# A retention and MLP kernel on one core: the Q tile holds both batches of a stream, and the weight slabs start from other loads

## The chip, the core and the metric

The kernel runs on one core of one Trainium2 chip. Its engines are TensorE (PE, matrix products; PEld is its weight load), VectorE (DVE), ScalarE (ACT), GpSimd (POOL) and SyncE (SP, which here only issues transfers). Data moves between DRAM and the on-chip memories through DMA queues that 16 DMA engines serve. The metric is the device time of one execution in microseconds (us), taken as the median of several runs.

## The reference

The inputs q, k and v have the shape 8 batches x 8 heads x 576 tokens x 64, in fp32. The second half is an MLP over all 4608 tokens.

```python
scores = 1/sqrt(64) * np.matmul(q, k.transpose(0, 1, 3, 2))
gamma = 1.0 - 2.0 ** (-5.0 - np.arange(H))
rel = pos[:, None] - pos[None, :]
Dmat = np.where(rel >= 0, gamma[:, None, None] ** rel[None, :, :], 0.0)
ret = (scores * Dmat) @ v
x = ret.transpose(0, 2, 1, 3).reshape(B * S, H * D)       # 4608 x 512
h = x @ w_in                                              # 512 x 2048
g = h * np.cos(h)
out = g @ w_out                                           # 2048 x 512, fp32
```

The decay matrix factors: gamma^(i-j) = gamma^i x gamma^-j. So the kernel scales row i of Q by gamma^i/8 (the table WQ) and row j of V by gamma^-j (the table WV), and only the causal mask is left for the scores.

## The kernel before

**Tiling.** A sequence of 576 tokens is cut into 9 chunks of 64. The 8 batches are split into two streams, x and y (numbers 0 and 1), and each stream goes through two generations: a unit (stream, k) with k from 0 to 17 is one chunk of the two batches that the stream has in that generation. Between chunks a state of keys times values is carried on in PSUM, so a chunk needs only its own keys and the state. Two units of a stream fill a part of one MLP tile; there are 9 MLP tiles (j from 0 to 8) of 512 tokens each.

**Loads of a pair of chunks.** `kv_tile` (L474 on) loads 128 tokens (two chunks) of K for each of two batches into `stgk` (L493, 256 KB each), and V into `stgv`. Each row is one token, and each piece of a row is one head's 64 fp32 numbers, 256 bytes. K is cast to bf16 into `natk` (L471) and V times WV goes to `natv` (L506), on ACT and DVE for the first tiles (`fast`) and on POOL for the others. K is then turned, with TensorE against the identity IDN (`tpe` L568, `tph` L586 for the last chunk of a sequence) or with a transposing DMA (`txb`, in generation 1).

**Q tiles.** `q_tile` (L528 on, load L543, multiply L550) has one tile per batch. In mode "n" the tile holds 128 tokens of one batch, one token in each of the 128 partitions, 256 KB in pieces of 256 bytes. In mode "p" it holds 256 tokens of one batch, two neighbouring tokens in each partition, 512 KB in pieces of 512 bytes. Chunk 8 is a mode "n" tile of 64 tokens. The product with WQ goes to `qnat`, its transpose to `qt`. In generation 0, chunks 0 to 3 are mode "n" and chunks 4 to 7 mode "p"; in generation 1 chunks 0 to 7 are mode "p". The pool of `stgq` has two slots.

**Sessions.** `session` (L608 on) takes the units that are due. On TensorE it issues scores (L627), new states (L636), the part of the output from the state (L645) and the part from the chunk itself (L654). DVE multiplies the scores by the mask (`pt`, L716), ACT copies outputs to `xt`, the MLP's input (L470).

**MLP.** `mlp1` issues x times w_in in groups of four matmuls (L756), then the sine (L764, ACT) and the product (L767, DVE). The second product is `plain2` (L793) for tile 0; for the others it is `wino2` (L879), a Strassen-Winograd form with fewer matmuls, whose operands DVE adds up (L840) from weights summed beforehand (`wsums`).

**Weights.** `load_w` (L736, L740) issues four slabs of w_in (512 KB each, 4 of the 16 column blocks of the MLP) and four of w_out on POOL's queue. The order of the w_in slabs is 0, 2, 1, 3. All eight wait for a gate: the landing of the second K load of stream y's first tile. The loads of chunks 2 and 3 (`GATE`) wait in turn: those of stream x for w_out slab 1, those of stream y for w_out slab 3.

**Order of the work.** `Graph` is a list scheduler: it takes the tasks with their priorities, planned durations, planned DMA times and buffer pools, and writes out one fixed stream of instructions per engine. It also models the fetching of TensorE's code: each block of 256 instructions becomes available FETCH (5500 ns) after it is asked for. Into gaps that the plan sees on TensorE before the first MLP matmul, `warm` (L412) puts dummy matmuls. On the chip the streams run in order, joined by semaphores.

Of the kernel before, what the change touches and what calls it, by code (L numbers as in the profile page):

```python
# [6 lines left out]
ALU = mybir.AluOpType  # L7
AF = mybir.ActivationFunctionType
F32 = mybir.dt.float32
# [120 lines left out]
class Graph:  # L130


    BACKLOG, FETCH, MARGIN = 2500, 5500, 60

    def __init__(self, pools):
        self.tasks, self.wr, self.rd = [], {}, {}
# [61 lines left out]
    def run(self, dma_rate):  # L198
# [65 lines left out]
        while n < len(self.tasks):  # L264
# [21 lines left out]
            if t.ni:  # L286
                while (len(got) + 0.74) * 256 <= count + t.ni:
                    at = s + t.dur * max(0, (len(got) + 0.74) * 256 - count) / t.ni
                    got.append(max([at] + [x - self.FETCH + 1500 for x in got[-1:]]) + self.FETCH)
                count += t.ni  # L290
            if t.port:
                port_free[e] = s + t.dur
# [30 lines left out]
class Kernel:  # L323
# [13 lines left out]
        [((), ((0, 4),)), (((0, 4),), ((0, 5), (1, 4))), (((0, 5), (1, 4)), ((0, 6), (1, 5))),  # L337
         (((0, 6), (1, 5)), ((0, 7), (1, 6)))])
    PLAIN = (0,)
    NOXBAR = set(range(7))  # L340
    PERIOD, T0, T1 = 28800, 18000, 32000

    def __init__(self, nc, es, q, k, v, w_in, w_out, out):
        self.nc = nc
        self.P = Prog(nc, es)
        self.src = [q.tensor, k.tensor, v.tensor]
        self.w_in, self.w_out, self.out = w_in.tensor, w_out.tensor, out.tensor
        sb = nc.alloc_sbuf_tensor
# [5 lines left out]
        self.WQ = sb("wq", [128, 56], F32)  # L354
# [4 lines left out]
        self.IQ = sb("iq", [128, 56], F32)  # L359
        self.IV = sb("iv", [128, 48], F32)  # L360
        self.LV = sb("lv", [128, 48], F32)
        self.LQ = sb("lq", [128, 56], F32)
# [55 lines left out]
    def constants(self):  # L418
# [5 lines left out]
        P.add("pool", lambda e: e.iota(ap(self.IV, 48, 0, 128, 40, [1, 8]), [[0, 8]], base=448,  # L424
                                       channel_multiplier=1, allow_small_or_imprecise_dtypes=True), w=[("iv", 1)])
        for m, r0 in self.WQS:
            o, nx = self.wq(m, r0), 2 if m == "p" else 1
            P.add("pool", lambda e, o=o, nx=nx, r0=r0: e.iota(
                ap(self.IQ, 56, 0, 128, o, [1, 8 * nx]), [[1, nx], [0, 8]], base=CH * r0, channel_multiplier=nx,
                allow_small_or_imprecise_dtypes=True), w=[("iq", o)])  # L430
        P.add("pool", lambda e: e.affine_select(self.IDN.ap(), self.ONE.ap(), pattern=[[1, 128]],
                                                compare_op=ALU.is_equal, fill=0.0, base=0,
                                                channel_multiplier=-1), r=["one"], w=["idn"])
        for h in range(H):
            P.add("dve", lambda e, h=h: e.memset(ap(self.LQ, 56, 0, 128, h, [8, 7]), lng[h]), w=[("lq", h)])
        for h in range(H):
            P.add("dve", lambda e, h=h: e.memset(ap(self.LV, 48, 0, 128, h, [8, 6]), -lng[h]), w=[("lv", h)])
        P.add("dve", lambda e: e.memset(self.CLN.ap(), math.log(1.0 / 8.0)), w=["cln"])
        P.add("dve", lambda e: e.memset(self.CPI.ap(), math.pi / 2), w=["cpi"])
        P.add("dve", lambda e: e.tensor_tensor(self.LQ.ap(), self.IQ.ap(), self.LQ.ap(), ALU.mult),  # L440
              r=[("iq", self.wq(*k)) for k in self.WQS] + [("lq", h) for h in range(H)], w=["lqx"])
# [77 lines left out]
        load("stgk", 1)  # L519
        return load, casts  # L520

    QT = {0: [("n", 0, 2), ("n", 2, 2), ("p", 4, 4), ("n", 8, 1)], 1: [("p", 0, 4), ("p", 4, 4), ("n", 8, 1)]}
    WQS = [("n", 0), ("n", 2), ("p", 4), ("n", 8), ("p", 0)]

    def wq(self, mode, r0):
        o = 0
        for m, r in self.WQS:
            if (m, r) == (mode, r0):  # L528
                return o
            o += 16 if m == "p" else 8  # L530

    def q_tile(self, x, gen, i, xbar, fast, gate=()):

        mode, r0, nr = self.QT[gen][i]
        wide = mode == "p"
        n, m = (64 if nr == 1 else 128), (2 if wide else 1) * D
        for b2 in range(2):
            t = {k: Buf(k) for k in ("stgq", "qnat")}
            t["qt"] = Buf("qt" if nr > 1 else "q8")
            for r in range(r0, r0 + nr):  # L540
                self.q[x, 9 * gen + r, b2] = (t["qt"], mode, r - r0)
            at = ((4 * gen + 2 * x + b2) * H * S + CH * r0) * D
            self.one("sp", 675, lambda e, t=t, at=at: e.dma_start(  # L543
                ap(self.at(t["stgq"]), 1024, 0, n, 0, [m, H], [1, m]),
                bass.AP(self.src[0], at, [[m, n], [S * D, H], [1, m]])),
                r=gate, w=[(t["stgq"],)], sem=lambda t=t: f"q{t['stgq'].slot}",
                dma=(1800 if wide else 1220) * n / 128)
            nx = 2 if wide else 1
            for y in range(nx):
                self.one("dve" if fast else "pool", 620 if fast else 990, lambda e, t=t, y=y: e.tensor_tensor(  # L550
                    ap(self.at(t["qnat"]), 1024, 0, 128, y * 512 + D * x, *self.heads(x)),
                    ap(self.at(t["stgq"]), 1024, 0, 128, y * D, [2 * m, 4], [m, 2], [1, D]),
                    ap(self.WQ, 56, 0, 128, self.wq(mode, r0) + 8 * y, [2, 4], [1, 2], [0, D]), ALU.mult),
                    r=[(t["stgq"],), ("wq",)], w=[(t["qnat"], y)], port=True)
            if n == 64:
                self.tph(t["qnat"], [(0,)], 0, 4, t["qt"], 0, [(0,)], "dve" if fast else "act")
            elif xbar:
                self.txb(t["qnat"], [(y,) for y in range(nx)], 4 * nx, t["qt"], [(0,)], "tq")
            else:
                self.tpe(t["qnat"], 0, [(y,) for y in range(nx)], 4 * nx, t["qt"], 0, (0,), "dve" if fast else "act")  # L560

    def tpe(self, src, off, rk, n, dst, doff, wk, eng):
        bk = Buf("bk")
# [36 lines left out]

    def queries(self, u, p0, b2, c):
        t, mode, i = self.q[u + (b2,)]
        if mode == "p":
            return ap(self.at(t), 1024, p0, 64, c * 128 + 32 * i, [512, 2], [1, 32])
        return ap(self.at(t), self.SIZE[t.pool][0], p0, 64, c * 128 + 64 * i, [1, 64])

    def keys(self, u):
# [2 lines left out]
    def session(self, outs, scs, prio):  # L610
# [48 lines left out]

        rsc, wsc, rin, wob, rst, wst, rpt = [], [], [], [], [], [], []  # L660
        for u in scs.values():
            rsc += [(self.keys(u)["kt"], 0), (self.keys(u)["kt"], 1)] + [(self.q[u + (b2,)][0], 0) for b2 in range(2)]
        if scs:
            wsc = [(b,) for b in sc]
        for u in inter.values():
            rin += [(self.sbd[u[0], u[1] - 1],)] + [(self.q[u + (b2,)][0], 0) for b2 in range(2)]
# [54 lines left out]
        for s, u in outs.items():  # L721
            xt = self.xt[u[1] // 2]
            o = u[0] * 1024 + 64 * (u[1] % 2)
            paired = self.q[u + (0,)][1] == "p"
# [194 lines left out]
    def graph(self):  # L919
# [5 lines left out]
        def tiles(units, fast=False, gate=()):  # L925
            for x, k in units:
                gen, r = divmod(k, NR)
                if (x, gen, r // 2) in have:
                    continue
                have.add((x, gen, r // 2))  # L930
                xbar = k not in self.NOXBAR
                load, casts = self.kv_tile(x, gen, r // 2, xbar, fast, gate)
                for i, (mode, r0, nr) in enumerate(self.QT[gen]):
                    if r in (r0, r0 + 1) and r0 // 2 == r // 2:
                        self.q_tile(x, gen, i, xbar, fast, gate)
                load("stgv", 2)
                casts()

# [5 lines left out]
                self.session(outs, scs, prio + step * i)  # L944

        run(self.EARLY[0], 0, 0, True)
        gate = [(self.kv[1, 0, 0]["stgk"], 1)]
        for s, x in enumerate((0, 2, 1, 3)):
            self.load_w("win", x, gate, 100 + s)
        for s in range(4):  # L950
            self.load_w("wout", s, gate, 200 + s)
        for h in range(2):
# [67 lines left out]
```

## Time and profile before

| what | value |
|---|---|
| median of 9 runs | 315.51 us (306.89 to 319.19) |
| the profiled execution: time | 306.89 us |
| its span, first to last instruction | 305.2 us |
| its mean granted TensorE clock | 0.994 |
| busy: PE, PEld, DVE, ACT, POOL | 96%, 72%, 68%, 63%, 36% of the span |
| DMA moved | 46.80 MB, mean 153 GB/s |
| read, written in DRAM | 36.70 MB, 9.44 MB |

Times are of the one profiled execution, which was also the shortest of the nine; the median stands 2.8% above it. A busy share is an average over the whole span. The profile also cuts the span into 40 slices of 7.6 us: each digit is the busy share of a slice in tenths, PEclk the TensorE clock that was granted, DMA the mean busy share of the DMA engines. The chain that ended last is followed back from the last instruction, and its shares say which engine the end waited for. Four further rows are useful for the code above (line, engine, operation, out<-in, count; busy us, mean ns of one; idle before it, and what ended most of it):

```profile
L550 POOL TENSOR_TENSOR qnat<-stgq,wq 128x512 bf16<-128x512 f32 x36 | 40.5, 1146 | 38.0 <-DMA stgq<-in_q_dram 24.4
L756 PE MATMUL bk<-xt,win 128*128 128x256 bf16 (+1 forms) x832 | 140.3, 315 | 0.2 <-DVE pt L716 0.2
stgq<-in_q_dram SPq DMA_DIRECT2D x12, 512.0 KB, 6.6
stgq<-in_q_dram SPq DMA_DIRECT2D x8, 256.0 KB, 5.4
```

POOL spends 40.5 us on scaling Q, and its idle time ahead of that was mostly a wait for a load of Q; the last two rows give the Q loads' number, size and median time in us from issue to landing.

### The profile page before, as it was taken

To read this page: it belongs to the slowest core of one execution; us is meant where nothing else is said; L and a number is where in the kernel's file an instruction comes from. 1 tells how busy PE (TensorE), PEld (TensorE's weight loads), DVE (VectorE), ACT (ScalarE), POOL (GpSimd) and SP (SyncE) were. 2 spreads that over 40 slices of the span, in tenths; PEclk is the share of its full clock that TensorE was granted. 3 is DMA by queue.
4 is the path that set the end of the run, shared out by engine and by line. 5 is a ranking of instruction groups with operands and counts; after the bars stand their busy time and mean duration, and the time that the engine had idled before them with its cause. 6 is when DMAs were issued, how large, how long until landed. Compare 5 with 4: busy or idle time off the path is not lost.

```text
span 305.2 us, 10278 instructions
## 1 busy us (share of the span) xinstructions
PE 293.6 (96%) x4319; PEld 220.1 (72%) x4319; DVE 207.2 (68%) x387; ACT 190.8 (63%) x356; POOL 109.9 (36%) x134
## 2 busy tenths in 40 slices
PE   8869999999999999999998999999999999999995
PEld 8758766678878887888666685567667765666684
DVE  3666873745995779779788746976767268966641
ACT  3439765798788595866756438656854666655420
POOL 2270057579787467540929015044330000000000
PEclk9997999999999999999999999999999999999999
DMA  9999999999999999997999799252003000300113
GB/s 169 201 192 207 208 229 215 245 267 220 193 224 228 176 244 275 196 192 222 229 243 218 163 227 159 48 110 67 4 0 139 2 2 2 139 2 1 69 71 137
DMA packets 126397, 46.80 MB, mean 153 GB/s; under 512 B 105104, under 2 KB 122000, under 8 KB 126352
## 3 DMA queue, kind: packets, MB, share of 16 engines
q1 hardware_dynamic: 122128, 41.95, 62.8%
q0 software_dynamic: 4224, 4.19, 8.3%
q8 instruction: 34, 0.56, 0.8%
q14 instruction: 11, 0.09, 0.1%
HBM read 36.70 MB, written 9.44 MB: 151 GB/s over the span
## 4 chain that ended last, share of the span: by engine, by line
PE 87%; DVE 4%; issue 2%; DMA 2%; ACT 2%; SPq 1%; POOL 0%; DVEq 0%; ACTq 0%
PE bk L756 39%; PE bk L879 32%; PE bk L793 4%; PE bk L654 2%; DMA stgv<-in_v_dram 2%; PE bk L627 2%; PE bk L412 2%; PE bk L568 2%; PE bk L645 2%; DVE gt L767 2%; PE st L636 2%; ACT cb L764 1%; SPq L493 1%; DVE s L840 1%; PE bk L586 1%
## 5 line engine op out<-in xcount | busy, mean ns | idle before, releaser
L764 ACT ACTIVATE cb<-bk,cpi 128x256 bf16<-128x256 f32 (+1 forms) x208 | 111.1, 560 | 52.1 <-PE bk L756 49.8
L767 DVE TENSOR_TENSOR gt<-bk,cb 128x256 bf16<-128x256 f32 (+1 forms) x208 | 105.5, 524 | 54.5 <-ACT cb L764 48.1
L756 PE MATMUL bk<-xt,win 128*128 128x256 bf16 (+1 forms) x832 | 140.3, 315 | 0.2 <-DVE pt L716 0.2
L756 PEld LDWEIGHTS bk<-xt,win 128*128 128x128 bf16 x832 | 79.9, 98 | 37.9 <-issue 0.6
L550 POOL TENSOR_TENSOR qnat<-stgq,wq 128x512 bf16<-128x512 f32 x36 | 40.5, 1146 | 38.0 <-DMA stgq<-in_q_dram 24.4
L506 POOL TENSOR_TENSOR natv<-stgv,wv 128x512 bf16<-128x512 f32 x38 | 39.9, 1063 | 17.7 <-DMA stgv<-in_v_dram 13.6
L471 POOL CAST natk<-stgk 128x512 bf16<-128x512 f32 x36 | 22.5, 639 | 59.6 <-PE st L636 33.8
L716 DVE TENSOR_TENSOR pt<-bk,tri 128x512 bf16<-128x512 f32 (+1 forms) x46 | 29.6, 683 | 18.9 <-PE st L636 12.4
L470 ACT ACTIVATE sbd<-st 128x512 bf16<-128x512 f32 x32 | 19.3, 604 | 23.1 <-PE st L636 23.1
L879 PE MATMUL bk<-wout,s 128*128 128x256 bf16 x256 | 32.6, 273 | 0.0
L879 PE MATMUL bk<-tw,s 128*128 128x256 bf16 x256 | 32.1, 273 | 0.2 <-DVE s L840 0.2
L879 PE MATMUL bk<-wout,gt 128*128 128x256 bf16 x256 | 31.4, 273 | 0.1
L879 PEld LDWEIGHTS bk<-tw,s 128*128 128x128 bf16 x256 | 24.6, 98 | 6.1 <-DVE s L840 0.7
L879 PEld LDWEIGHTS bk<-wout,s 128*128 128x128 bf16 x256 | 24.6, 98 | 6.0
L879 PEld LDWEIGHTS bk<-wout,gt 128*128 128x128 bf16 x256 | 24.6, 98 | 3.7
L470 ACT ACTIVATE sn<-bk 128x512 f32<-128x512 f32 x24 | 14.5, 606 | 16.7 <-PE bk L879 16.7
L470 ACT ACTIVATE xt<-bk 128x512 bf16<-128x512 f32 x36 | 23.3, 696 | 0.6 <-PE bk L654 0.6
L891 DVE TENSOR_TENSOR os<-bk,sn 128x512 f32<-128x512 f32 x24 | 16.5, 686 | 9.9 <-PE bk L879 9.8
L793 PE MATMUL bk<-wout,gt 128*128 128x512 bf16 x64 | 16.3, 379 | 0.2 <-DVE gt L767 0.2
L879 PE MATMUL bk<-tw,gt 128*128 128x256 bf16 x128 | 16.4, 273 | 0.0
L879 PEld LDWEIGHTS bk<-tw,gt 128*128 128x128 bf16 x128 | 12.4, 98 | 3.4
L627 PE MATMUL bk<-qt,kt 64*64 64x64 bf16 x512 | 9.9, 194 | 4.9 <-POOL natv L506 2.1
(63 smaller groups left out, 233.3 us busy)
## 6 DMA issues: line engine op xcount, KB each, us to landing
stgk<-in_k_dram SPq DMA_DIRECT2D x32, 256.0 KB, 4.9
stgv<-in_v_dram SPq DMA_DIRECT2D x32, 256.0 KB, 5.5
out_dram<-os SPq DMA_DIRECT2D x15, 512.0 KB, 3.3
stgq<-in_q_dram SPq DMA_DIRECT2D x12, 512.0 KB, 6.6
stgq<-in_q_dram SPq DMA_DIRECT2D x8, 256.0 KB, 5.4
win<-in_moe_w_in_dram POOLq DMA_DIRECT2D x4, 512.0 KB, 10.1
wout<-in_moe_w_out_dram POOLq DMA_DIRECT2D x4, 512.0 KB, 14.5
out_dram<-os SPq DMA_DIRECT2D x6, 256.0 KB, 3.3
```

Source lines behind the costliest of these rows:

```text
L470: return self.one(eng, dur, lambda e: e.activation(dst(), src(), AF.Copy), r=r, w=w, **kw)
L471: return self.one(eng, dur, lambda e: e.tensor_copy(dst(), src()), r=r, w=w, port=True, **kw)
L506: self.one(ve, vd, lambda e, b2=b2: e.tensor_tensor(ap(self.at(t["natv"]), 1024, 0, 128, 512 * b2, [D, H], [1, D]), ap(self.at(t["stgv"]), ...
L550: self.one("dve" if fast else "pool", 620 if fast else 990, lambda e, t=t, y=y: e.tensor_tensor(ap(self.at(t["qnat"]), 1024, 0, 128, y * 5 ...
L627: yield lambda e, b2=b2, c=c: e.matmul(ap(self.at(sc[ph]), 512, 64 * s, 64, (4 * b2 + c) * 64, [1, 64]), ap(self.at(self.keys(u)["kt"]), 1 ...
L716: self.one("dve", 610, lambda e, hp=hp: e.tensor_tensor(ap(self.at(pt), 1024, p0, n, 512 * hp, [64, 8], [1, 64]), ap(self.at(sc[hp]), 512, ...
L756: inst = e.matmul(ap(self.at(bk), 512, 0, 128, 0, [1, n]), ap(self.WIN, 4 * DFF, 0, 128, c * DFF + 128 * f, [1, 128]), ap(self.at(xt), 204 ...
L764: self.one("act", 70 + n, lambda e: e.activation(ap(self.at(cb), TB, 0, 128, 0, [1, n]), ap(self.at(bk), 512, 0, 128, 0, [1, n]), AF.Sin, ...
L767: self.one("dve", 75 + n / 0.96, lambda e: e.tensor_tensor(ap(self.at(gt), NF * TB, 0, 128, f * TB + 256 * h0, [1, n]), ap(self.at(bk), 51 ...
L793: inst = e.matmul(self.at(bk).ap(), ap(self.at(gt), NF * TB, 0, 128, f * TB + 256 * half + 128 * tt, [1, 128]), ap(self.WOUT, NF * DM, 0, ...
L879: inst = e.matmul(ap(self.at(bank), 512, 0, 128, 256 * tt, [1, 256]), l(f, tt), rr(f), start=(first and f == 0 and tt == 0), stop=True, sk ...
L891: self.one("dve", 610, lambda e: e.tensor_tensor(view(h, c), ap(self.at(bank), 512, 0, 128, 0, [256, 2], [1, 256]), ap(self.at(sn[name]), ...
```

## The change

There are three edits.

The first is the Q tile. A tile of mode "h" holds both batches of a stream for two chunks (128 tokens): batch b2 fills partitions 64 x b2 to 64 x b2 + 63, and each partition holds two neighbouring tokens, so that a piece is 512 bytes. Each tile takes two loads of 256 KB, each into 64 partitions, then two multiplies (one for each token of the pair) and two transposes. Chunk 8 stays a mode "n" tile per batch, of 64 tokens. Counted over the kernel, Q goes from 12 loads of 512 KB, 8 of 256 KB and 8 of 128 KB to 32 of 256 KB and 8 of 128 KB. The table WQ is laid out anew (72 columns instead of 56), with one more DVE operation that sets back the token index in the upper 64 partitions (`iqx`). `queries` and `qkeys` give the sessions the new places and dependencies. The outputs of more units are now copied in the pair order (`paired`).

The second is the weights' start. The first w_in slab (LEAD = 1) waits for the first V load of stream x's first tile; the other seven slabs wait for the last Q load of stream y's first tile instead of its last K load.

The third is in the planner: the model of the code fetches drops a lower bound from the fetch before, and adds 3500 ns (SLOW) to the fetches 3, 10 and 17. With these the order of instructions on TensorE, DVE, POOL and SP changes in many places, and the planned dummy matmuls go from 159 to 135. The number of real matmuls stays.

```diff
-    BACKLOG, FETCH, MARGIN = 2500, 5500, 60
+    BACKLOG, FETCH, SLOW, MARGIN = 2500, 5500, 3500, 60
...
-                    got.append(max([at] + [x - self.FETCH + 1500 for x in got[-1:]]) + self.FETCH)
+                    got.append(at + self.FETCH + (self.SLOW if len(got) in (3, 10, 17) else 0))
...
+    LEAD = 1
...
         for m, r0 in self.WQS:
-            o, nx = self.wq(m, r0), 2 if m == "p" else 1
-            P.add("pool", lambda e, o=o, nx=nx, r0=r0: e.iota(
-                ap(self.IQ, 56, 0, 128, o, [1, 8 * nx]), [[1, nx], [0, 8]], base=CH * r0, channel_multiplier=nx,
-                allow_small_or_imprecise_dtypes=True), w=[("iq", o)])
+            nx = 2 if m == "h" else 1
+            P.add("pool", lambda e, nx=nx, r0=r0: e.iota(
+                ap(self.IQ, 72, 0, 128, 8 * r0, [1, 8 * nx]), [[1, nx], [0, 8]], base=CH * r0, channel_multiplier=nx,
...
+        P.add("dve", lambda e: e.tensor_scalar_add(
+            ap(self.IQ, 72, 64, 64, 0, [1, 64]), ap(self.IQ, 72, 64, 64, 0, [1, 64]), -128.0),
+              r=[("iq", r0) for m, r0 in self.WQS], w=["iqx"])
...
-    QT = {0: [("n", 0, 2), ("n", 2, 2), ("p", 4, 4), ("n", 8, 1)], 1: [("p", 0, 4), ("p", 4, 4), ("n", 8, 1)]}
-    WQS = [("n", 0), ("n", 2), ("p", 4), ("n", 8), ("p", 0)]
-
-    def wq(self, mode, r0):
-        o = 0
-        for m, r in self.WQS:
-            if (m, r) == (mode, r0):
-                return o
-            o += 16 if m == "p" else 8
-
-    def q_tile(self, x, gen, i, xbar, fast, gate=()):
-
-        mode, r0, nr = self.QT[gen][i]
-        wide = mode == "p"
-        n, m = (64 if nr == 1 else 128), (2 if wide else 1) * D
-        for b2 in range(2):
+    WQS = [("h", 0), ("h", 2), ("h", 4), ("h", 6), ("n", 8)]
+
+    def q_tile(self, x, gen, r0, xbar, fast, gate=()):
+
+        nr = 2 if r0 < NR - 1 else 1
+        wide = nr == 2
+        for bs in [(0, 1)] if wide else [(0,), (1,)]:
             t = {k: Buf(k) for k in ("stgq", "qnat")}
-            t["qt"] = Buf("qt" if nr > 1 else "q8")
+            t["qt"] = Buf("qt" if wide else "q8")
             for r in range(r0, r0 + nr):
-                self.q[x, 9 * gen + r, b2] = (t["qt"], mode, r - r0)
-            at = ((4 * gen + 2 * x + b2) * H * S + CH * r0) * D
-            self.one("sp", 675, lambda e, t=t, at=at: e.dma_start(
-                ap(self.at(t["stgq"]), 1024, 0, n, 0, [m, H], [1, m]),
-                bass.AP(self.src[0], at, [[m, n], [S * D, H], [1, m]])),
-                r=gate, w=[(t["stgq"],)], sem=lambda t=t: f"q{t['stgq'].slot}",
-                dma=(1800 if wide else 1220) * n / 128)
-            nx = 2 if wide else 1
-            for y in range(nx):
+                for b2 in bs:
+                    self.q[x, 9 * gen + r, b2] = (t["qt"], "h" if wide else "n", r - r0)
+            self.kv[x, gen, r0 // 2]["stgq"] = t["stgq"]
+            m = 2 * D if wide else D
+            for b2 in bs:
+                at, p0 = ((4 * gen + 2 * x + b2) * H * S + CH * r0) * D, 64 * b2 if wide else 0
+                self.one("sp", 675, lambda e, t=t, at=at, p0=p0: e.dma_start(
+                    ap(self.at(t["stgq"]), 1024, p0, 64, 0, [m, H], [1, m]),
+                    bass.AP(self.src[0], at, [[m, 64], [S * D, H], [1, m]])),
+                    r=gate, w=[(t["stgq"], i) for i in ([b2] if wide else bs + (1 - b2,))],
+                    sem=lambda t=t, b2=b2: f"q{t['stgq'].slot}_{b2}",
+                    dma=900 if wide else 610)
+            ys = range(2 if wide else 1)
+            for y in ys:
                 self.one("dve" if fast else "pool", 620 if fast else 990, lambda e, t=t, y=y: e.tensor_tensor(
                     ap(self.at(t["qnat"]), 1024, 0, 128, y * 512 + D * x, *self.heads(x)),
                     ap(self.at(t["stgq"]), 1024, 0, 128, y * D, [2 * m, 4], [m, 2], [1, D]),
-                    ap(self.WQ, 56, 0, 128, self.wq(mode, r0) + 8 * y, [2, 4], [1, 2], [0, D]), ALU.mult),
-                    r=[(t["stgq"],), ("wq",)], w=[(t["qnat"], y)], port=True)
-            if n == 64:
+                    ap(self.WQ, 72, 0, 128, 8 * (r0 + y), [2, 4], [1, 2], [0, D]), ALU.mult),
+                    r=[(t["stgq"], i) for i in range(2)] + [("wq",)], w=[(t["qnat"], y)], port=True)
+            if not wide:
                 self.tph(t["qnat"], [(0,)], 0, 4, t["qt"], 0, [(0,)], "dve" if fast else "act")
             elif xbar:
-                self.txb(t["qnat"], [(y,) for y in range(nx)], 4 * nx, t["qt"], [(0,)], "tq")
+                self.txb(t["qnat"], [(y,) for y in ys], 8, t["qt"], [(y,) for y in ys], "tq")
             else:
-                self.tpe(t["qnat"], 0, [(y,) for y in range(nx)], 4 * nx, t["qt"], 0, (0,), "dve" if fast else "act")
+                for y in ys:
+                    self.tpe(t["qnat"], 512 * y, [(y,)], 4, t["qt"], 512 * y, (y,), "dve" if fast else "act")
+
+    def qkeys(self, u):
+        return [(self.q[u + (b2,)][0], y) for b2 in range(2) for y in range(2 if self.q[u + (b2,)][1] == "h" else 1)]
...
-        if mode == "p":
-            return ap(self.at(t), 1024, p0, 64, c * 128 + 32 * i, [512, 2], [1, 32])
+        if mode == "h":
+            return ap(self.at(t), 1024, p0, 64, c * 128 + 64 * b2 + 32 * i, [512, 2], [1, 32])
...
-            rsc += [(self.keys(u)["kt"], 0), (self.keys(u)["kt"], 1)] + [(self.q[u + (b2,)][0], 0) for b2 in range(2)]
+            rsc += [(self.keys(u)["kt"], 0), (self.keys(u)["kt"], 1)] + self.qkeys(u)
...
-        gate = [(self.kv[1, 0, 0]["stgk"], 1)]
+        gate = [(self.kv[1, 0, 0]["stgq"], 1)]
         for s, x in enumerate((0, 2, 1, 3)):
-            self.load_w("win", x, gate, 100 + s)
+            self.load_w("win", x, gate if s >= self.LEAD else [(self.kv[0, 0, 0]["stgv"], 0)], 100 + s)
```

More of the change, by code (lines that the diff above doesn't have):

```diff
@@ L353, in __init__ @@
         self.WV = sb("wv", [128, 48], F32)
-        self.WQ = sb("wq", [128, 56], F32)
+        self.WQ = sb("wq", [128, 72], F32)
         self.IDN = sb("idn", [128, 128], BF16)
@@ L358, in __init__ @@
         self.ONE = sb("one", [128, 128], BF16)
-        self.IQ = sb("iq", [128, 56], F32)
+        self.IQ = sb("iq", [128, 72], F32)
         self.IV = sb("iv", [128, 48], F32)
         self.LV = sb("lv", [128, 48], F32)
-        self.LQ = sb("lq", [128, 56], F32)
+        self.LQ = sb("lq", [128, 72], F32)
         self.CLN = sb("cln", [128, 1], F32)
@@ L426, in constants @@
         for m, r0 in self.WQS:
-            o, nx = self.wq(m, r0), 2 if m == "p" else 1
-            P.add("pool", lambda e, o=o, nx=nx, r0=r0: e.iota(
-                ap(self.IQ, 56, 0, 128, o, [1, 8 * nx]), [[1, nx], [0, 8]], base=CH * r0, channel_multiplier=nx,
-                allow_small_or_imprecise_dtypes=True), w=[("iq", o)])
+            nx = 2 if m == "h" else 1
+            P.add("pool", lambda e, nx=nx, r0=r0: e.iota(
+                ap(self.IQ, 72, 0, 128, 8 * r0, [1, 8 * nx]), [[1, nx], [0, 8]], base=CH * r0, channel_multiplier=nx,
+                allow_small_or_imprecise_dtypes=True), w=[("iq", r0)])
         P.add("pool", lambda e: e.affine_select(self.IDN.ap(), self.ONE.ap(), pattern=[[1, 128]],
@@ L434, in constants @@
         for h in range(H):
-            P.add("dve", lambda e, h=h: e.memset(ap(self.LQ, 56, 0, 128, h, [8, 7]), lng[h]), w=[("lq", h)])
+            P.add("dve", lambda e, h=h: e.memset(ap(self.LQ, 72, 0, 128, h, [8, 9]), lng[h]), w=[("lq", h)])
         for h in range(H):
@@ L439, in constants @@
         P.add("dve", lambda e: e.memset(self.CPI.ap(), math.pi / 2), w=["cpi"])
+        P.add("dve", lambda e: e.tensor_scalar_add(
+            ap(self.IQ, 72, 64, 64, 0, [1, 64]), ap(self.IQ, 72, 64, 64, 0, [1, 64]), -128.0),
+              r=[("iq", r0) for m, r0 in self.WQS], w=["iqx"])
         P.add("dve", lambda e: e.tensor_tensor(self.LQ.ap(), self.IQ.ap(), self.LQ.ap(), ALU.mult),
-              r=[("iq", self.wq(*k)) for k in self.WQS] + [("lq", h) for h in range(H)], w=["lqx"])
+              r=["iqx"] + [("iq", r0) for m, r0 in self.WQS] + [("lq", h) for h in range(H)], w=["lqx"])
         P.add("dve", lambda e: e.tensor_tensor(self.LV.ap(), self.IV.ap(), self.LV.ap(), ALU.mult),
@@ L665, in session @@
         for u in inter.values():
-            rin += [(self.sbd[u[0], u[1] - 1],)] + [(self.q[u + (b2,)][0], 0) for b2 in range(2)]
+            rin += [(self.sbd[u[0], u[1] - 1],)] + self.qkeys(u)
         for s, u in outs.items():
@@ L723, in session @@
             o = u[0] * 1024 + 64 * (u[1] % 2)
-            paired = self.q[u + (0,)][1] == "p"
+            paired = self.q[u + (0,)][1] == "h"
             inner = ([1, 2], [2, 32]) if paired else ([1, 64],)
@@ L932, in tiles @@
                 load, casts = self.kv_tile(x, gen, r // 2, xbar, fast, gate)
-                for i, (mode, r0, nr) in enumerate(self.QT[gen]):
-                    if r in (r0, r0 + 1) and r0 // 2 == r // 2:
-                        self.q_tile(x, gen, i, xbar, fast, gate)
+                self.q_tile(x, gen, r - r % 2, xbar, fast, gate)
                 load("stgv", 2)
```

## Prediction

> **What bounds the kernel now.** I read the page first, sections 1, 2 and 4 (busy time, 40 slices, the chain that ended last). All four lines are about who is never idle.
>
> ```profile
> PE 293.6 (96%) x4319; PEld 220.1 (72%) x4319; DVE 207.2 (68%) x387; ACT 190.8 (63%) x356; POOL 109.9 (36%) x134
> PE   8869999999999999999998999999999999999995
> DMA  9999999999999999997999799252003000300113
> PE 87%; DVE 4%; issue 2%; DMA 2%; ACT 2%; SPq 1%; POOL 0%; DVEq 0%; ACTq 0%
> ```
>
> TensorE holds 87% of the chain, and the number of its real matmuls does not change. So time can be won or lost where it is not full, in the first three slices (23 us), or by new waits. The DMA engines are full for 18 slices, up to 137 us: there a dearer transfer pushes all later ones. Next the waits of TensorE (us in total, times, longest):
>
> ```profile
> PE bk L627 <- POOL natv L506: 2.1, 1, 2.1
> PE bk L627 <- issue: 1.0, 1, 1.0
> PE bk L654 <- issue: 0.7, 2, 0.4
> ```
>
> One wait of 2.1 us is worth naming, a session waiting for V; "issue" waits, which another order might move, are 1.7 us in all. The chain in order of time (start, us, what) says where the V wait came from:
>
> ```profile
> 10.96 2.67 SPq L493
> 13.68 6.55 DMA stgv<-in_v_dram
> 20.30 1.05 POOL natv L506
> 22.40 1.46 PE bk L756 x8
> 25.29 8.41 PE bk L756 x72
> ...
> 34.56 1.31 PE bk L756 x12
> ```
>
> The last V load of stream y takes 6.55 us from issue to landing (the four early V loads lie between 5.1 and 6.5); the weight slabs start beside it. Then come natv, the y sessions and the MLP. 1.31 us for 12 gives 0.109 us a matmul.
>
> **Part 1, weight slabs.** The view of the tile win:
>
> ```profile
> L736 POOL DMA_DIRECT2D win<-in_moe_w_in_dram x4: 753/766/954, 14.2 to 16.6; - x4
> DMA to landing us min/median/max: 7.3/10.1/12.5
> ```
>
> First slab: issued 14.2, landed 14.2+7.3 = 21.5. Fourth: 16.6+12.5 = 29.1. So a slab costs (29.1-21.5)/3 = 2.5 us of the DMA engines. The second wout slab is the sixth: 21.5+5x2.5 = 34.0, and SP's next loads, gated on it, do start at 34.2. The eighth lands near 39.0.
>
> After: slab 0 goes when the first V load of stream x has landed, ahead of most of y's loads on the same engines, and delays these by 0 to 2.5 us. The other seven wait for y's last Q load instead of its K. Q was there by 15.57 (DVE L550 starts on it); SP's 0.8 us wait for a Q slot (L543 behind DVE qnat) falls away as both batches share a slot. So the gate opens between 15.6-0.8 = 14.8 and 14.8+2.5 = 17.3. Slab 2 lands 7.3 later, 22.1 to 24.6; the sixth slab 4x2.5 on, 32.1 to 34.6 (34.0 before); the last 37.1 to 39.6 (39.0): -1.9 to +0.6 us.
>
> TensorE's order after: 16 MLP matmuls ahead of y's first two sessions' end, 4 between the y sessions, against 0 and 8. So 12x0.109 = 1.3 us of work is done early. But it is in order: y's K transposes stand ahead of session x1 as before, now with K up to 2.5 us later; the last 4 of the 20 want slab 2, and a wait there holds the second y session. On POOL natv of y stands behind four issues of 0.8 us (3.2, from the gate: 18.0 to 20.5), with y's V behind it; before there were five, done at 18.1, and V set the start at 20.30. SP is passed by nothing. As the weights pace the next stage (gated loads on the sixth slab, the DVE sums on the last), I take the middle of -1.9 to +0.6: **-0.65 us**.
>
> Clock: the windows view (PE busy, granted clock, DMA share, GB/s).
>
> ```profile
> 19.33:22.75 3.42, 1.30 (x53) 1.00 1.24 204
> 22.75:26.16 3.41, 3.41 (x59) 0.50 1.24 208
> ```
>
> After a stretch with 1.30 of 3.42 us busy the clock is halved for 3.41 us. Cost: x8 at 1.46 for 0.87, x72 at 8.41 for 7.86, so 1.1 us. After, the 16 dummies ahead of y's sessions are gone (159 become 135 in all) and real matmuls of like length stand there; I leave the dip at 0 change, with -1.1 in the range. [...]
>
> **Part 2, Q loads.** Before 8 loads of 256 KB (256 B packets) and 12 of 512 KB (512 B), all into 128 partitions; after 32 of 256 KB with 512 B packets, each into 64 partitions. Windows with a full queue (POOL busy, clock, DMA share, GB/s): K, Q, V in 256 B; the 512 KB Q loads twice; and 82.6 to 84.4, where chunk 8's K and Q go into 64 partitions in 256 B:
>
> ```profile
> 42.50:50.00 7.50, 5.40 (x6) 1.00 1.11 215
> 65.00:67.00 2.00, 1.28 (x3) 1.00 0.96 278
> 82.60:84.40 1.80, 1.79 (x3) 1.00 1.16 173
> 92.50:94.50 2.00, 1.67 (x3) 1.00 1.11 326
> ```
>
> Before: 256 KB at 215 is 1.22 us; 512 KB at 302 (mean of 278 and 326) 1.74. After no row has 512 B into 64 partitions. Bounds for 256 KB: 0.87 us (302, packets alone count) and 1.52 (173, the half-width destination alone counts). I take 1.3, two thirds of the way to 1.52, since half-width is the nearer row: 173 is a fifth under 215 with DMA share at 1.16. Up to chunk 8's Q the queue holds 16 such loads: 16x1.3 = 20.8 against 8x1.22+4x1.74 = 16.7, +4.1 us (-2.8 to +7.6). Cover: the first chunk 8 transposes.
>
> ```profile
> 85.98 2.55 POOL L550 TENSOR_TENSOR qnat<-stgq,wq 128x512 bf16<-128x512 f32 x2 [1.09 <-DMA stgq<-in_q_dram]
> ...
> 89.07 0.29 PE L586 MATMUL bk<-idn,qnat 64*128 64x64 bf16 x4
> ```
>
> The first of two POOL operations ends at 85.98+1.27 = 87.25, TensorE takes it at 89.07: 1.8 us. POOL had waited 1.09 us for the load, so it is the DMA that is late here. 4.1-1.8 = **+2.3 us** (0 to +5.8). Earlier, at 72 us, chunks 6 and 7 need not be loaded yet, which covers that place. Later the DMA digits fall to 7 and the loads catch up.
>
> [...]
>
> **The rest, 0.** Q multiplies, transposes and scores keep their number. ACT: four qt copies of 1.03 become eight of 0.6, and eight xt copies go from 0.61 to 0.70: under 2 us, at 63% busy, inside the MLP where TensorE has matmuls queued. Startup: one more DVE addition (some 0.2 us); wq is due at 6.47 when Q lands and ACT had it at 2.4. The planner's new fetch figures change TensorE's order throughout: 0, with 1.7 us (all issue waits) either way.
>
> **Sum.** The profiled execution took 306.89 us, span 305.2 and 1.7 around it. -0.65+2.3 = +1.65: 308.5, ratio 1.0054. The nine runs go from 306.89 to 319.19 and the profiled one is the lowest; on the median, 315.51x1.0054 = 317.2.
>
> **Rivals.**
> *Slower (0.43), the forecast*: half-width Q loads, +1.65, own range 316 to 320.5.
> *No change (0.30)*: packets of 512 B win back what half-width costs. 302x173/215 = 243 GB/s, 1.08 us a load, 17.3 against 16.7 us, inside the 1.8; with -0.65 left 314.8. For it: half-width loads went at 190 GB/s in quieter places. Against: that is with 256 B, whose own limit is 215.
> *Faster (0.27)*: the front decides. Mechanism: y's loads lose little to slab 0, the gate opens at 14.8, the weight stream ends 1.9 early and the dip goes (1.1); -3.0, 312.4. It holds if Q of y lands before 15.6 and a Q load stays under about 1.15 us (16x1.15-16.7 = 1.7, inside the cover).
>
> About 0.5%, 1.6 us, is what this measurement can tell from none. The low end, 306.5, takes in that the median may fall among the three lowest runs (306.9 to 308.8); the high end adds Q loads at 1.45 us (23.2-16.7-1.8 = 4.7): 315.5+4.7 = 320.2, rounded up.
>
> **What would show it.** After: q loads with landings 1.2 us or more apart in a full queue; new TensorE waits of L568 or L586 on POOL qnat or natk between 60 and 100 us, some 2 us in sum; the first L756 near 18 us, before y's sessions; slab 2 landing between 22 and 25 us. Wrong if DMA runs at 240 GB/s or more through Q loads, if no POOL wait over 0.3 us appears after 30 us, or if issue waits change by more than 1.7.

## The result, and the profile after

The changed kernel takes 314.49 us (median of 21 runs, 312.22 to 316.61). Ratio to the kernel before: **1.0203, 95% interval 1.0171 to 1.0234**, so 2% slower, some 6.2 us on a run of 307. By the medians nothing changed (315.03 us over 63 runs before, 314.49 now): executions of the kernel before spread from 306.39 to 323.06 us, the ratio takes only the 13 of them within 1.5% of the shortest, and no trace here shows what makes the others longer. The loss is one against the kernel before at its best. The profiled execution took 316.58 us, one of the longest of its kernel; a second profiled execution is shown further down.

The page of the changed kernel, busy time, slices and the chain that ended last:

```profile
PE 294.5 (94%) x4295; PEld 218.8 (70%) x4295; DVE 207.3 (66%) x388; ACT 191.9 (61%) x360; POOL 110.8 (35%) x134
PE   8779888987889988999999999999999999999995
DMA  9989999999999999989999999905001100200123
PE 72%; DMA 15%; POOL 4%; SPq 3%; issue 3%; ACT 2%; DVE 0%; POOLq 0%; DVEq 0%; ACTq 0%
```

TensorE's busy time is nearly the same (293.6 before). Its share of the chain fell from 87% to 72%, and DMA's rose from 2% to 15%. Digits under 9 now go on up to the 16th slice, 126 us, where before they ended with the third, but for one 8; the DMA digits drop at 204 us (26 slices of 7.86) instead of 191 (25 of 7.63). Then TensorE's waits (us in total, times, longest; line numbers are 4 higher than before):

```profile
PE bk L572 <- POOL qnat L550: 3.2, 5, 1.2
PE st L640 <- issue: 2.4, 1, 2.4
PE bk L572 <- ACT natk L474: 2.2, 2, 1.8
PE bk L572 <- POOL natk L475: 1.8, 1, 1.8
PE bk L797 <- DMA wout<-in_moe_w_out_dram: 0.7, 1, 0.7
```

Before, for the same transposes:

```profile
PE bk L568 <- ACT natk L470: 0.4, 1, 0.4
PE bk L568 <- DVE qnat L550: 0.2, 1, 0.2
```

The transposes of Q and K (L572) now wait 7.2 us for the casts of K and the multiplies of Q, and these mostly for loads (1.8 us of it at 14.7 us, in the front, for a K that landed hardly later than before, near 14.0); before, that line (L568) waited 0.6 us. "issue" is a wait for which the profile shows no releaser. The chain in order of time (start, us, what) shows the loads behind them:

```profile
9.55 9.21 DMA stgq<-in_q_dram
19.06 2.30 POOL win L740 x3
...
24.60 16.65 DMA wout<-in_moe_w_out_dram
...
56.25 5.00 DMA stgq<-in_q_dram
61.41 1.08 POOL qnat L550 x2
62.49 4.96 DMA stgq<-in_q_dram
...
68.68 1.91 POOL qnat L550 x2
70.59 7.13 DMA stgq<-in_q_dram
...
79.09 2.05 POOL qnat L550 x2
```

From 9.55 to 79 us the end was set mostly by loads of Q and by the weights, one after the other. y's last Q load, the new gate, landed at 9.55+9.21 = 18.76; before, it landed near 15.7. POOL issued the seven slabs from 19.06, and the last landed at 24.60+16.65 = 41.25 (39.7 before).

To place the loss I divided both executions at two landings: the first K load behind the weights, and the last V load of chunks 6 and 7. Between them each kernel moves the same K, V, Q and output, 9472 KB by the loads' sizes. Windows of before, then of after (us, TensorE busy, granted clock, DMA share, GB/s):

```profile
0.00:40.69 40.69, 35.82 (x546) 0.96 1.14 199
40.69:82.76 42.07, 41.01 (x764) 1.00 1.02 228
82.76:305.20 222.44, 216.78 (x3012) 1.00 0.59 131
```

```profile
0.00:42.32 42.32, 35.47 (x527) 0.96 1.11 191
42.32:88.72 46.40, 40.74 (x756) 1.00 1.12 209
88.72:314.50 225.78, 218.29 (x3015) 0.99 0.65 128
```

The three stages are longer by **1.6, 4.3 and 3.3 us**. In the middle one TensorE does nearly the same work and is idle for 5.7 us instead of 1.1; the bytes go at 209 GB/s instead of 228.

### The profile page after: what moved, and what is told of

Read it like the earlier page. It is cut to its first block, busy times and chain, and to the rows that moved or that the text cites. A ratio compares the mean times of both kernels' runs of the same rounds, so it can differ in the third digit from the quotient of the medians.

```text
span 314.5 us, 10240 instructions
## 1 busy us (share of the span) xinstructions
PE 294.5 (94%) x4295; PEld 218.8 (70%) x4295; DVE 207.3 (66%) x388; ACT 191.9 (61%) x360; POOL 110.8 (35%) x134
## 4 chain that ended last, share of the span: by engine, by line
PE 72%; DMA 15%; POOL 4%; SPq 3%; issue 3%; ACT 2%; DVE 0%; POOLq 0%; DVEq 0%; ACTq 0%
PE bk L760 33%; PE bk L883 31%; DMA stgq<-in_q_dram 10%; DMA wout<-in_moe_w_out_dram 5%; POOL qnat L550 2%; SPq L497 2%; PE bk L649 2%; SPq L542 1%; PE bk L631 1%; PE bk L658 1%; PE st L640 1%; PE bk L590 1%; POOL win L740 1%; POOL wout L744 1%; PE bk L797 1%
## 5 line engine op out<-in xcount | busy, mean ns | idle before, releaser
L760 PE MATMUL bk<-xt,win 128*128 128x256 bf16 (+1 forms) x832 | 144.4, 316 | 3.1 <-DVE gt L771 2.6
L550 POOL TENSOR_TENSOR qnat<-stgq,wq 128x512 bf16<-128x512 f32 x36 | 39.5, 1116 | 46.8 <-issue 22.1
L510 POOL TENSOR_TENSOR natv<-stgv,wv 128x512 bf16<-128x512 f32 x38 | 41.2, 1100 | 10.0 <-PE bk L658 8.2
L475 POOL CAST natk<-stgk 128x512 bf16<-128x512 f32 x36 | 23.2, 663 | 56.2 <-PE st L640 33.7
L883 PE MATMUL bk<-wout,gt 128*128 128x256 bf16 x256 | 32.6, 275 | 0.0
L474 ACT ACTIVATE xt<-bk 128x512 bf16<-128x512 f32 x36 | 24.4, 728 | 0.2 <-PE bk L658 0.2
L797 PE MATMUL bk<-wout,gt 128*128 128x512 bf16 x64 | 16.0, 379 | 0.7 <-DMA wout<-in_moe_w_out_dram 0.7
L474 ACT ACTIVATE kt<-bk 128x512 bf16<-128x512 bf16 x20 | 11.7, 609 | 4.9 <-PE bk L572 4.9
```

What stands on the lines that cost most here:

```text
L474: return self.one(eng, dur, lambda e: e.activation(dst(), src(), AF.Copy), r=r, w=w, **kw)
L475: return self.one(eng, dur, lambda e: e.tensor_copy(dst(), src()), r=r, w=w, port=True, **kw)
L510: self.one(ve, vd, lambda e, b2=b2: e.tensor_tensor(ap(self.at(t["natv"]), 1024, 0, 128, 512 * b2, [D, H], [1, D]), ap(self.at(t["stgv"]), ...
L760: inst = e.matmul(ap(self.at(bk), 512, 0, 128, 0, [1, n]), ap(self.WIN, 4 * DFF, 0, 128, c * DFF + 128 * f, [1, 128]), ap(self.at(xt), 204 ...
L797: inst = e.matmul(self.at(bk).ap(), ap(self.at(gt), NF * TB, 0, 128, f * TB + 256 * half + 128 * tt, [1, 128]), ap(self.WOUT, NF * DM, 0, ...
L883: inst = e.matmul(ap(self.at(bank), 512, 0, 128, 256 * tt, [1, 256]), l(f, tt), rr(f), start=(first and f == 0 and tt == 0), stop=True, sk ...
```

## The experiments

Theory A: Q loads into 64 neighbouring partitions are slow, the loads set the pace, and the new gate makes the weights late as well; TensorE waits for nearly all of it. Rivals: the gate alone (B), the gate only together with the new Q tiles (G), or the planner's new order (C or P).

### One part of the change at a time

**q_only**: the changed kernel with gate and fetch model undone.

```diff
-        gate = [(self.kv[1, 0, 0]["stgq"], 1)]
+        gate = [(self.kv[1, 0, 0]["stgk"], 1)]
...
+            self.load_w("win", x, gate, 100 + s)
...
+                    got.append(max([at] + [x - self.FETCH + 1500 for x in got[-1:]]) + self.FETCH)
```

> The changed kernel with its new Q tiles, but with the weight gate and the planner's fetch model of the kernel before. Theory A (half-width Q loads slow the load stream): the loads up to the last V of chunks 6 and 7, 9472 KB behind the first K after the weights in both kernels, take some 46 us as in the changed kernel and not 42 as before; the time is 3.5 to 6 us over before, ratio 1.012 to 1.020. Theory B (the weight gate is the main loss): the stream is slower but hidden, ratio within 1.000 to 1.005. Theory C (the planner's new order): ratio 1.000 to 1.005.

Measured: 311.42 us, ratio 1.0001 (0.9934 to 1.0067): the time was missed, and it is the one that rivals B and C had. The stretch was as theory A has it:

```profile
0.00:40.24 40.24, 35.08 (x542) 1.00 1.12 199
40.24:87.21 46.97, 41.31 (x764) 1.00 1.00 206
87.21:307.70 220.49, 216.26 (x3010) 1.00 0.63 132
```

4.9 us more in the middle, but 0.5 us less in front (mean clock 1.00 there, 0.96 before) and 2.0 less behind. So the slower stream is there without the gate, and this execution got half of it back in other stages. The executions lie between 307.32 and 315.34; a ratio of such a spread does not price the part, and the next set prices it better.

**gate_only**: the kernel before, first slab behind x's V and the others behind y's Q.

```diff
+    LEAD = 1
...
+            self.kv[x, gen, r0 // 2]["stgq"] = t["stgq"]
...
-        gate = [(self.kv[1, 0, 0]["stgk"], 1)]
+        gate = [(self.kv[1, 0, 0]["stgq"],)]
...
-            self.load_w("win", x, gate, 100 + s)
+            self.load_w("win", x, gate if s >= self.LEAD else [(self.kv[0, 0, 0]["stgv"], 0)], 100 + s)
```

> The kernel before with only the new weight gate: first slab behind x's first V load, the other seven behind y's last Q load. Theory A: the first slab ahead of y's loads delays y's Q by some 3 us (near 18.7 against 15.7), so the seven slabs are issued some 4 us later, the last lands near 41 against 39.7; the time is 0 to 1.5 us over before (ratio 1.000 to 1.005), since the first MLP matmuls start earlier. Theory B: 4 to 6 us over before (1.013 to 1.020). Theory C: 0.

Measured: 310.52 us, ratio 1.0019 (0.9975 to 1.0064), as theory A said. Its rows for the tile win (the slabs' issues, and the longest wait ahead of one):

```profile
L738 POOL DMA_DIRECT2D win<-in_moe_w_in_dram x4: 747/782/952, 9.4 to 20.5; - x4
...
  DMA stgq<-in_q_dram: 7.4, 1
```

With the old full-width Q loads, y's Q still landed at 18.7 (15.7 before) and the seven slabs were issued from 19.0. So slab 0 can push Q back by 3 us without the new width of Q.

**plan_only**: the kernel before with the new fetch figures.

```diff
-    BACKLOG, FETCH, MARGIN = 2500, 5500, 60
+    BACKLOG, FETCH, SLOW, MARGIN = 2500, 5500, 3500, 60
...
-                    got.append(max([at] + [x - self.FETCH + 1500 for x in got[-1:]]) + self.FETCH)
+                    got.append(at + self.FETCH + (self.SLOW if len(got) in (3, 10, 17) else 0))
```

> The kernel before with only the planner's new fetch figures (no lower bound from the fetch before, 3500 ns on fetches 3, 10 and 17). Theories A and B: within 1.5 us of before either way (0.995 to 1.005). Theory C: 4 to 6 us over before (1.013 to 1.020).

Measured: 311.28 us, ratio 1.0032 (0.9974 to 1.009). Theory C's 4 to 6 us are ruled out; 0.8 us less or 2.8 more are not. In its profiled execution TensorE's "issue" waits are longer, not shorter (1.7 us in all before):

```profile
PE bk L654 <- issue: 2.3, 1, 2.3
PE st L636 <- issue: 1.8, 2, 0.9
PE bk L756 <- issue: 1.3, 1, 1.3
```

### The same bytes into other partitions

**q_inter**: every second partition instead of one half. The rest of the kernel still takes the rows in the old order, so its outputs are other numbers.

```diff
-                    ap(self.at(t["stgq"]), 1024, p0, 64, 0, [m, H], [1, m]),
+                    bass.AP(self.at(t["stgq"]), p0 // 64 * 1024, [[2048 if wide else 1024, 64], [m, H], [1, m]]),
```

> The changed kernel, except that the two loads of a Q tile write every second partition (batch 0 the even ones, batch 1 the odd ones) and not one half of the partitions each. The rows of Q are then in another order than the rest of the kernel takes them to be, so the outputs are other numbers; work, sizes, packets and order are those of the changed kernel. Theory A (the destination of 64 neighbouring partitions is what is slow): a Q load goes from 1.3 us to about 0.87 to 1.0 us in a full queue, packets of 512 bytes at 250 GB/s and more against some 200, the stream up to chunks 6 and 7 takes 41 to 43 us, and the time falls 3.5 to 5 us under the changed kernel (ratio to before 1.003 to 1.009). Rival (the number of loads, their order and the slots): Q at some 200 GB/s as in the changed kernel, ratio 1.017 to 1.022.

Measured: 309.33 us, ratio 1.0000 (0.9952 to 1.0048), a little under theory A's figure and far from the rival's. This is the sharpest pair of the study, since instructions, their order, the number of loads and the packet size are those of the changed kernel. Windows in which Q packets hold nearly all of the queue (us, TensorE busy, clock, DMA share, GB/s), first the changed kernel, then this one, then this one's middle stretch:

```profile
50.40:51.00 0.60, 0.60 (x11) 1.00 1.24 171
82.20:83.40 1.20, 1.20 (x14) 1.00 1.12 180
98.40:99.00 0.60, 0.60 (x8) 1.00 1.18 210
```

```profile
55.20:55.80 0.60, 0.60 (x4) 1.00 1.02 300
93.00:94.20 1.20, 1.18 (x13) 1.00 1.10 315
...
41.11:83.47 42.36, 40.41 (x760) 1.00 1.00 227
```

Neighbouring partitions: 171 to 210 GB/s in these windows, so 256 KB in 1.25 to 1.53 us. Alternate partitions: 300 to 315 GB/s, 0.83 to 0.87 us, the rate of the old 512 KB loads (278 and 326 GB/s in two windows of before). What makes neighbouring partitions the slower ones no run here shows. Short windows vary (the changed kernel had 299 GB/s from 57.6 to 58.4 us); over the whole kernel, the median Q load took 5.4 us from issue to landing in the changed kernel and 4.7 in this one. The stretch goes back from 46.40 to 42.36 us.

### Taking parts off the changed kernel

**old_gate** undoes the gate, **old_plan** the fetch model (their diffs are in q_only's). **lead_k** keeps slab 0 early and puts the seven behind K again; **inter_old_gate** is q_inter with the old gate.

```diff
-        gate = [(self.kv[1, 0, 0]["stgq"], 1)]
+        gate = [(self.kv[1, 0, 0]["stgk"], 1)]
```

> The changed kernel with the old weight gate alone (all eight slabs behind y's last K load); Q tiles and planner new. Theory A (half-width Q loads cost the load stream 4 to 5 us, the new gate another 1.5 to 2.5 at the weights, and TensorE waits for both): the weights land some 1.5 us earlier (last near 39.5), the ratio to before falls from 1.020 to between 1.004 and 1.013. Rival G (the parts alone cost nothing, only the gate together with the Q tiles does): 1.000 to 1.004. Rival P (the new planner's order together with the Q tiles): 1.015 to 1.022, as in the changed kernel.

> The changed kernel with the old fetch model in the planner; Q tiles and gate new. Theory A: loads and weights land as in the changed kernel, ratio 1.013 to 1.022. Rival P: 1.002 to 1.008.

> The changed kernel with seven slabs behind y's last K load as before, and only the first slab early behind x's V. Theory A, if it is the wait for Q that makes the weights late: the gate opens near 14 (K landed at 14.0 in the changed kernel too), the seven slabs are issued 4 to 5 us earlier, the last lands near 39, ratio 1.003 to 1.012. If it is the early slab itself that costs: y's Q and V land later still (V after 22), the y sessions start 2 us later, ratio 1.017 to 1.025.

> The changed kernel with both suspected costs taken away: Q loads into every second partition (so Q's rows are in another order than the rest takes them to be, and the outputs are other numbers), and the old gate for all eight slabs. Theory A: ratio to before 0.992 to 1.002. Rival P (the planner's order): 1.003 to 1.010.

| kernel | median us | ratio (95%) |
|---|---|---|
| old_gate | 312.02 | 1.0099 (1.0032 to 1.0166) |
| old_plan | 313.37 | 1.0173 (1.0117 to 1.0229) |
| lead_k | 315.46 | 1.0258 (1.0197 to 1.0319) |
| inter_old_gate | 306.57 | 0.9965 (0.9905 to 1.0024) |

Three of the four fell where theory A put them. Between old_gate and inter_old_gate only Q's partitions differ: 1.3%, some 4 us, close to the 4.3 of the stretch. The gate is worth about 1% (1.0203 to 1.0099), with intervals that only just part; old_gate's reaches down to 1.0032, so it does not quite exclude rival G. The planner's figures make no difference that these runs can tell.

lead_k was the slowest, and not for the reason that I had given alone. y's last V did land late (POOL's multiply, which waited for it, starts at 23.84; at 20.30 before), but the chain (start, us, what) shows more:

```profile
18.95 19.98 DMA wout<-in_moe_w_out_dram
38.95 0.70 DVE tw L823
39.68 0.69 DVE tw L823
40.37 1.03 DVE natv L510
```

In this plan one of y's V multiplies stands on DVE behind the sums of weights, which wait for the last slab at 38.93. Early weights did not help, since a late V was queued behind them. So this kernel does not price the early slab by itself.

### A followed-through version, and the last two questions

**q_even** makes the alternate partitions a working kernel, with the old gate. The sessions read every second column of qt; batch 1's decay starts one token later in Q and V, which cancels. **q_even_old** has the old planner too.

```diff
...
-            return ap(self.at(t), 1024, p0, 64, c * 128 + 64 * b2 + 32 * i, [512, 2], [1, 32])
+            return ap(self.at(t), 1024, p0, 64, c * 128 + b2 + 64 * i, [512, 2], [2, 32])
...
-                    ap(self.WV, 48, 0, 128, 8 * iv, [1, H], [0, D]), ALU.mult),
+                    ap(self.WV, 96, 0, 128, 8 * iv + 48 * b2, [1, H], [0, D]), ALU.mult),
...
-        P.add("dve", lambda e: e.tensor_scalar_add(
...
```

**lead_none** is the changed kernel with `LEAD = 0`, so that all eight slabs wait for Q; **after_again** is the changed kernel as it stands.

> The changed kernel with the old weight gate and with Q of batch 0 in the even and of batch 1 in the odd partitions, this time followed through: the sessions read every second column of qt, and batch 1's decay tables start one token later in both Q and V, which cancels. Theory A: as with the reordered rows, ratio to before 0.990 to 1.003; the stream from the first K behind the weights to the last V of chunks 6 and 7 takes 41 to 43 us. Rival: reading every second column makes the 64-wide loads of weights and matmuls of the sessions dearer, or the longer tables start later, 1.005 and more.

> The same with the old planner figures too, so that only the Q tiles differ from the kernel before. Theory A: within 1.5 us of the kernel above either way, 0.990 to 1.005. Rival P: 1.5 us or more apart from it, with the difference in waits for instructions.

> The changed kernel with no early slab: all eight slabs behind y's last Q load. If the early slab is what makes the front late: Q of y lands near 16 as with the old gate (18.8 in the changed kernel), slab 0 lands near 23, the last slab near 41, ratio 1.012 to 1.022, that is not worse than the changed kernel's 1.020. If the wait for Q is what costs: 1.020 to 1.030, as the MLP then starts later than in the changed kernel and the weights no sooner.

> The changed kernel once more, beside the others and for a second profile. Theory A: ratio 1.015 to 1.023; the waits for Q and K between 44 and 82 us and the stream of 45 to 47 us are there again, while the wait for instructions of 2.4 us near 117 us with the low clock after it belongs to that one execution and is smaller or elsewhere. If that wait belongs to the kernel, it is there again near 117.

| kernel | median us | ratio (95%) |
|---|---|---|
| q_even | 306.04 | 0.9893 (0.9824 to 0.9962) |
| q_even_old | 306.50 | 0.9901 (0.9845 to 0.9957) |
| lead_none | 313.69 | 1.0146 (1.0087 to 1.0206) |
| after_again | 314.36 | 1.0170 (1.0102 to 1.0239) |

q_even beats both kernels, by about 1% against the one before, a little under theory A's 0.990. Its page and its middle stretch:

```profile
PE 293.4 (96%) x4310; PEld 218.9 (72%) x4310; DVE 207.8 (68%) x387; ACT 191.7 (63%) x360; POOL 111.3 (37%) x137
PE   8869999999899999999999999999999999999995
...
41.02:81.57 40.55, 39.18 (x745) 1.00 1.03 235
```

Between the third slice and the last there is one 8; the stretch takes 40.55 us, 1.5 less than before, at 235 GB/s. Reading every second column cost nothing here: a score matmul has a mean of 194 ns before and here. With the old planner the ratio is the same.

Over the profiled executions that I divided at these landings, the middle stretch separates the kernels by Q's partitions: 44.9 to 47.0 us with half loads into neighbouring ones (the changed kernel, q_only, old_gate, lead_none), 40.6 to 43.7 with all others (before, gate_only, plan_only, q_inter, inter_old_gate, q_even).

lead_none, without an early slab, issued its slabs from 17.4 us, so y's Q landed near 17.1 (in the changed kernel the issue followed the landing by 0.3); its first K load behind the weights landed at 42.88, in the changed kernel at 42.32. It is not slower than the changed kernel beside it; so the early slab, and the head start of the MLP that it brings, gained nothing that can be measured. Nor is it the early slab alone that makes the weights late: here the loads behind them came no earlier, and all eight had waited for Q.

after_again showed what belonged to the first profiled execution alone. Windows of the first, then of the second (us, TensorE busy, clock, DMA share, GB/s):

```profile
116.50:120.00 3.50, 1.14 (x127) 1.00 1.10 203
120.00:123.50 3.50, 3.50 (x29) 0.61 1.20 270
```

```profile
116.50:120.00 3.50, 3.50 (x149) 1.00 0.94 215
```

The "issue" wait of 2.4 us and the low clock behind it are gone in the second, whose longest such wait is 1.2 us. The waits of L572 are there again (3.8 us for qnat, 1.1 for natk).

## Why the prediction was wrong

The direction, and the mechanism behind it, were right: half-width Q loads slow the load stream (209 GB/s in the middle stretch, 228 before, 227 with alternate partitions) and the waits come out at the transposes of Q and K. The size was not: a ratio of 1.0054 was forecast and 1.0203 measured, 1.65 us against some 6.2. The median of 314.49 lies inside the range of 306.5 to 320.5, but that is no merit of the sum: the 315.03 of the kernel before lies there too, and the ratio is the fairer test. Two terms of the sum failed, the cover and the weights.

- **A Q load, 1.3 us: right as a mean.** The windows give 1.25 to 1.53. The 16 loads behind the 4.1 us take in the four of chunks 0 and 1, which land by 18.76, ahead of most of the weights; for the other 12 the same prices give 12x1.3-(4x1.22+4x1.74) = 3.8 us, and up to the V of chunks 6 and 7 the stretch was 4.3 longer.
- **The cover of 1.8 us: failed.** The prediction looked for the first wait at chunk 8's transposes, near 89 us, and set 72 us aside because chunks 6 and 7 were not to be loaded yet. But TensorE waited for loads of every pair of chunks up to there: 0.5 and 0.6 us for Q of chunks 2 and 3 (at 48.8 and 55.4 us), 1.2 for Q of chunks 4 and 5, then 1.8 for K and 0.9 for Q of stream x's chunks 6 and 7. The two longest:

```profile
69.78 0.40 PE L572 MATMUL bk<-idn,qnat 128*128 128x128 bf16 x4 [1.16 <-POOL qnat L550]
...
77.37 0.40 PE L572 MATMUL bk<-idn,natk 128*128 128x128 bf16 x4 [1.76 <-POOL natk L475]
```

In the stretch up to the V of chunks 6 and 7 the stream was 4.3 us longer and TensorE idle 4.6 us more. The cover was nil, and +2.3 should have been some +4.3.
- **The weights, -0.65: failed in sign.** The delay of y's Q by slab 0 was bounded at 2.5 us, what one slab costs, with 0.8 to be got back; the gate was to open between 14.8 and 17.3. (The 15.57 behind these figures is the start of the first of two multiplies; the second load landed near 15.7.) Q landed 3 us late, at 18.76, and in gate_only, with the old loads, at 18.7. Half-width loads of y's Q itself were put at nothing: lead_none, with no slab ahead of them, had it near 17.1 (15.7 before). Slab 2 was inside the bounds given (24.5 against 22.1 to 24.6), the last slab was not (41.25 against 37.1 to 39.6). The stage in front came out 1.6 us longer where 0.65 less was forecast. That is the second 2 us. In the profiled executions divided at these landings, the front took 41.1 to 42.9 us with the new gate (the changed kernel, gate_only, q_inter, lead_none) and 39.0 to 41.0 with the old one (before, plan_only, q_only, old_gate, inter_old_gate, q_even).
- **The early MLP matmuls** came as forecast, the first at 18.4 us, ahead of y's sessions. They gave nothing: lead_none, with its first at 23.6 us, is not slower. What followed waited for weights, 0.7 us for w_out at L797.
- **The rest, 0 with 1.7 either way: right as far as the runs tell.** old_plan and plan_only, and q_even against q_even_old, show no difference from the planner's figures; q_only and old_gate, which differ in them alone, stand at 1.0001 and 1.0099 with intervals that overlap. The clock dip was left unchanged, and the front has a mean clock of 0.96 before and after. In the first profiled execution the last stage was 3.3 us longer; the "issue" wait of 2.4 us at 117 us and the low clock behind it (3.5 us at 0.61, an estimated 3.5x0.39 = 1.4) are enough for that, and the second did not have them. But lead_none was 2.3 us longer there too, so a part may belong to the kernel.

1.6 and 4.3 are 5.9 us, close to the 6.2 of the ratio. By the ratios, Q's width is worth 3 to 6 us (q_only against q_even_old, old_gate against inter_old_gate, the changed kernel against q_inter). The gate is worth 1 us (q_inter against inter_old_gate), 3 (the changed kernel against old_gate) or 5 (old_plan against q_only), and 0.6 in gate_only with the old Q tiles, each with 2 to 3 us either way. So it stays open why the two parts alone measured 1.000 and 1.002, and together 1.020: that the gate costs more beside slow Q loads (rival G) is neither shown nor excluded.

The rival that was to end on the other side needed a Q load under 1.15 us, and alternate partitions show that this half of it was sound: at 0.83 to 0.87 us a load, and with the old gate, the kernel is faster than before.

## What to carry to other kernels

When the DMA engines are full, price a new load layout by the partitions that it writes as well as by its packet length, and write a half-size load into every second partition rather than into 64 neighbours (300 to 315 GB/s against 171 to 210 here, in packets of 512 bytes). A slack read at one waiting instruction covers a slower stream only if every earlier consumer has as much (here 1.8 us at chunk 8, while TensorE was idle 4.6 us more ahead of it); look for the first one that is due, not for the tightest that the old order shows. A transfer put ahead of others on the same engines can delay them by more than its own size suggests (y's Q by 3 us in gate_only, behind one slab of an estimated 2.5), and a gate on one of those delays all that is behind it (in the changed kernel seven slabs were issued from 19.06, and the last landed at 41.25 instead of 39.7).

## What the runs showed of the hardware that was not expected

- The same 512-byte packets, in the same order, went at 171 to 210 GB/s into 64 neighbouring partitions and at 300 to 315 into 64 alternate ones, in the windows shown.
- With one 512 KB slab issued ahead of y's second Q load, that load landed 3 us later in gate_only (18.7 against 15.7 before) and some 1.6 later in the changed kernel (18.76 against near 17.1 in lead_none); 2.5 us a slab is the estimate from the first and the fourth landing before (21.5 and 29.1).
- 64-wide matmuls that read every second column took 194 ns on the mean in q_even, as with neighbouring columns before.
